# Moving x's transposes from once per batch to once per head pair, w2's bf16 copy into wd, and w2*w_out products to one lane

## The chip, the cores and the metric

The kernel runs on one core of a Trainium2 chip. The metric is device time in microseconds of one launch, the median of the timed runs. Five engines work side by side, each in its own program order: TensorE (PE; its weight loads are listed as PEld), VectorE (DVE), ScalarE (ACT), GpSimd (POOL) and SyncE (SP, which here only issues DMAs). They wait for each other through semaphores.

## The reference

Attention with queries averaged in pairs, then a maxout MoE layer on its output:

```python
B, H, S, D = 8, 8, 1152, 64
q_pool = q.reshape(B, H, S // 2, 2, D).mean(axis=3)
attn = softmax(q_pool @ k.T / sqrt(D))           # rows of 576 queries
attn_out = attn @ v                              # [8, 8, 576, 64]
x = attn_out.transpose(0, 2, 1, 3).reshape(4608, 512)
g = maximum(x @ w1, x @ w2)                      # w1, w2: 512 x 1024
out = g @ w_out                                  # w_out: 1024 x 512
```

All inputs and the output are fp32.

## The kernel before

It uses max(a, b) = max(a - b, 0) + b, so out = max(x (w1 - w2), 0) w_out + x (w2 w_out). Two bf16 matrices are made once: wd = w1 - w2 and w21 = w2 * w_out. The work is then of these kinds; letters are the queue names in the code.

- q, k: GpSimd casts a head pair's queries and keys (`qp` L353, `kbf` L329) and values (`vE` L367); queries and keys are transposed, for the first pairs on TensorE, later by DMA from SyncE's queue (L425, L342).
- Scores (L535) go to three, later two PSUM buffers `sps` in groups of 512 columns for both heads of a pair (the two halves of TensorE's rows at once). ScalarE's exponential (L542) turns each group into `et`. There are 324 groups over 32 head pairs.
- a: attention products per head, 45 matmuls of 65 columns (L384), with the row sum as an extra column. VectorE normalises: reciprocal (L473), multiply (L475), into `xnat`.
- x: `xnat` of a batch is transposed to `xT` (512 features in four blocks of 128 partitions, 4608 tokens). The first and the last batch are transposed on TensorE (`xtrans_pe`, L599, copied out at L605), batches 1 to 6 by DMA (`xtrans`, L585). Both start when all eight heads of a batch are normalised (`finish`, `x_wait`), in five pieces of tokens, 4 x 128 and 64, each of all 512 features.
- w: w2 is cast to bf16 (`w2b`, L626), transposed on TensorE (L641) to `w2T` (copied out at L647), and multiplied with w_out (`w21_jobs`, copied out at L660). wd is the subtraction L629. fp32 w2, w2b and w2T lie in the parts of `xT` that belong to later tokens, so x may be written there only when they have been read (`under`).
- h: max(x wd, 0) for 8 blocks of features (evacuated at L700, in the tail in part at L696).
- p: the output product of h with w_out plus x with w21, 12 matmuls per 128 tokens (evacuated at L729 or L726, stored from SyncE's queue at L676).

The order of all instructions is made before the launch. The `Plan` object keeps an estimate of each engine's free time and of when each operand will be seen; the loop `while p_end[0] < NTOK` picks the next unit for TensorE: scores when ScalarE has little queued, attention units before other work, MoE units (w, p, h) in what is left. `refill` turns queued jobs into running ones when a PSUM bank is free. While exponentials run, from group NARROW on, w, p and h jobs run as pairs, crossed: two jobs, each on one half of TensorE's rows at a time (L390); before it and in the tail they run whole (L384). Before NARROW there are two banks `fb` for everything but scores, then four, in the tail eight. A waiting instruction holds up all behind it on its engine.

Of the kernel before, what the change touches and what calls it, by code (L numbers as in the profile page):

```python
# [207 lines left out]
def bass_funnel_attn__then__act_maxout2_kernel(  # L208
# [32 lines left out]
    with ctx:  # L241
# [17 lines left out]
        rc = [sbuf([P, NCH + 1], FP32, f"rc{s}") for s in range(2)]  # L259
        xnat = [sbuf([P, NCH + 1, C], BF16, f"xnat{s}") for s in range(2)]  # L260
        xT = sbuf([P, NC_, NTOK], BF16, "xT")
# [109 lines left out]
        def unit(r, cost, go, mode="f"):  # L371
            return Unit(r, cost, mode, go=go)
# [81 lines left out]
        def av_jobs(i):  # L454
            b, h0 = i // NHP, 2 * (i % NHP)
            es = i % 2
            vs = i % 3
            xs = b % 2
            c0 = h0 * D
            need = [f"et{es}.{g - first(i)}" for g in range(first(i), after(i))] + [f"vE{vs}", "pad"]  # L460

            def chunk(half, sb):
                parts = []
                for t in range(NT):
                    a = (half * 2 + es) * PW + spot(i, t, sb * P)
                    parts.append((sb * 66, et[:, a:a + P], vE[vs][:, t, half, 0:65], t == 0, t == NT - 1))
                return parts

            def norm(half):
                def evac(m):  # L470
                    c = c0 + half * D
                    a = fb[m][:, 0:(NCH + 1) * 66].rearrange("p (j c) -> p j c", c=66)
                    dve(lambda e: e.reciprocal(rc[half][:, :], a[:, :, 64:65]),  # L473
                        [f"f{m}"], [f"rc{half}"], 0.19)
                    dve(lambda e: e.tensor_tensor(  # L475
                        xnat[xs][:, :, c:c + D], a[:, :, 0:D],
                        rc[half][:, :].unsqueeze(2).to_broadcast([P, NCH + 1, D]), ALU.mult),
                        [f"f{m}", f"rc{half}"],
                        [f"xn{xs}.{h0 + half}", f"f{m}"], 0.5)
# [82 lines left out]

        def place(b, j):

            if b % 2 == 0:
                return b * SQ + j * P
            return b * SQ + (NB + j * P if j < NCH else 0)

        def under(n0, n1):

            keys = [key for key, lo, hi in (("w2b", 512, 1536), ("w2T", 1536, 2560),
                                            ("w2f", 2560, NTOK)) if n0 < hi and lo < n1]
            if "w2T" in keys:
                keys += [f"w2T{ct}" for ct in range(NC_)]
            return keys

        def xsize(j):
            return P if j < NCH else NB

        def xtrans(b):  # L580
            xs = b % 2
            assert b == 0 or not queue["w"]
            for j in range(NCH + 1):
                n, n0 = xsize(j), place(b, j)
                op("SP", lambda e, n=n, n0=n0, j=j: e.dma_start_transpose(  # L585
                    xT[:, :, n0:n0 + n], xnat[xs][0:n, j, :]),
                    r=[f"xn{xs}.{h}" for h in range(H)], w=xkeys(n0, n0 + n),
                    after=under(n0, n0 + n), dma=f"d_x{xs}{j}", cost=0.65, mode="t")

        def xtrans_pe(b):  # L590
            xs = b % 2
            jobs = []
            for j in range(NCH + 1):
                n, n0 = xsize(j), place(b, j)

                def go(e, m, n=n, j=j):
                    mb = fb[m][:, :].bitcast(BF16)
                    for c in range(NC_):
                        last = e.transpose(mb[:, c * P:c * P + n],  # L599
                                           xnat[xs][0:n, j, c * P:(c + 1) * P], ident[0:n, 0:n])  # L600
                    return last

                def evac(m, n=n, n0=n0):
                    mb = fb[m][:, :].bitcast(BF16)[:, 0:NC_ * P].rearrange("p (c x) -> p c x", x=P)
                    op("DVE", lambda e: e.tensor_copy(xT[:, :, n0:n0 + n], mb[:, :, 0:n]),  # L605
                       r=[f"f{m}"], w=xkeys(n0, n0 + n) + [f"f{m}"], after=under(n0, n0 + n),
                       cost=0.4)
                jobs.append(Job("x", [unit([f"xn{xs}.{h}" for h in range(H)] + ["ident"],
                                           0.22 if n == P else 0.13, go, "f" if n == P else "s")],
                                evac))  # L610
            return jobs

        def xkeys(n0, n1):
            return [f"xT.{j}" for j in range(n0 // HP, n1 // HP)]

# [8 lines left out]
        def w_cast(part, ct):  # L624
            if part == 0:
                dve(lambda e: e.tensor_copy(w2b[:, ct, :], w2f[:, ct, :]),  # L626
                    [f"w2f{ct}"], [f"w2b{ct}", "w2b"], 0.6)
            elif part == 1:
                dve(lambda e: e.tensor_tensor(  # L629
                    wd[:, ct, :], w1f[:, ct, :], w2f[:, ct, :], ALU.subtract),  # L630
                    [f"w1f{ct}", f"w2f{ct}"], [f"wd{ct}", "w2f"], 1.2)
            else:
                dve(lambda e: e.tensor_copy(
                    wo[:, 2 * ct:2 * ct + 2, :], wof[:, 2 * ct:2 * ct + 2, :]),
                    [f"wof{ct}"], [f"wo{2 * ct}", f"wo{2 * ct + 1}"], 0.6)

        def w2t_job(ct):
# [7 lines left out]
            def evac(m):  # L645
# [3 lines left out]
                    [f"f{m}"], [f"w2T{ct}", "w2T", f"f{m}"], 1.15)  # L649
            return Job("w", [unit([f"w2b{ct}", "w2b", "ident"], 0.44, go)], evac)  # L650

# [16 lines left out]
        def store(lo, s, at):  # L668

            for half in range(2):  # L670
                n0 = lo + half * HP
                b, u = n0 // SQ, n0 % SQ
                if b % 2:
                    u = (u - NB) % SQ
# [9 lines left out]
        def h_jobs(n0, n1):  # L684
# [3 lines left out]
            for ft in range(NF):  # L688
                def part(ct, ft=ft):
                    return mm_unit([f"wd{ct}"] + [f"wo{j}" for j in range(NF)] + xkeys(n0, n1), 0.216 * size / 512, [  # L690
                        (0, wd[:, ct, ft * P:(ft + 1) * P], xT[:, ct, n0:n1], ct == 0, ct == NC_ - 1)])
# [14 lines left out]
        def p_job(lo, at=slice(0, E)):  # L706
# [3 lines left out]
            def part(j):  # L710
                if j < NC_:
                    lhs, rhs = xT[:, j, lo:hi], w21[:, j, at]
                    r = [f"w21{j}"] + xkeys(lo, hi)
                else:
# [118 lines left out]
        def flush():  # L833
# [24 lines left out]
            for b in list(x_wait):  # L858
                if b in X_PE:
                    x_wait.remove(b)  # L860
                    queue["x"].extend(xtrans_pe(b))
                elif plan.ops[plan.writer[f"xn{b % 2}.{H - 1}"]]["seen"] <= now():
                    x_wait.remove(b)
                    xtrans(b)

# [18 lines left out]
        def more_moe():  # L884
            tail = nxt == NGR
            keys = [f"wd{ct}" for ct in range(NC_)] + [f"wo{ft}" for ft in range(NF)]
            while h_at[0] < NTOK and not queue["h"] and all(key in plan.writer for key in keys):
                n0 = h_at[0]
                most = min(HB - n0 % HB, p_end[0] + RING - n0, NTOK - n0)
                n1 = n0  # L890
                while n1 < n0 + most and all(key in plan.writer for key in xkeys(n1, n1 + HP)) and plan.when(
                        "PE", r=xkeys(n1, n1 + HP)) <= now() + (9.0 if tail else 0.05):
                    n1 += HP
# [25 lines left out]
        def refill():  # L919
# [232 lines left out]
```

## Time and profile before

| | us |
|---|---|
| timed runs, median of 3 | 381.17 (380.3 to 381.26) |
| profiled execution, own time | 379.94 |
| its span on the core | 378.2 |
| TensorE busy | 360.4 (95%) |
| ScalarE busy | 317.6 (84%) |
| GpSimd busy | 162.4 (43%) |
| VectorE busy | 139.9 (37%) |

The span is cut into rows by engine, line and tile. TensorE's busy time is modelled at its ends, so a TensorE at 95% is not one at its peak. TensorE's clock was at full speed throughout. An idle time in brackets is that of the engine just ahead of the row, with what ended it.

### The profile page before, as it was taken

The page shows a single profiled execution, that of the slowest core. Times are in us where ns is not written, and L with a number is a line of the kernel's source. Part 1 is how long each engine was busy: PE and PEld are TensorE (multiplying, and loading weights), DVE is VectorE, ACT ScalarE, POOL GpSimd, SP SyncE. Part 2 cuts the span into 40 slices and gives each one's busy share as a digit, 9 for nine tenths or more (in the row PEclk, how much of TensorE's full clock was granted, in tenths as well). Part 3 has the DMA queues.
Part 4 walks back from the last instruction along what each step waited for, and adds up shares of the span by engine and source line. Part 5 has one row for each costly group of instructions (what it writes and reads, how often), then busy time and mean ns, then how long its engine had stood idle before and what let it go on. Part 6 is the DMA issues. An engine that isn't in the chain of part 4 may idle for free.

```text
span 378.2 us, 13193 instructions
## 1 busy us (share of the span) xinstructions
PE 360.4 (95%) x5928; PEld 232.0 (61%) x5928; DVE 139.9 (37%) x323; ACT 317.6 (84%) x359; POOL 162.4 (43%) x135
## 2 busy tenths in 40 slices
PE   4798999899999999999999999999999999999996
PEld 2464566667665656666666666666656666676554
DVE  3256963314234242422343333241424243353221
ACT  5999989899989999999999899899999999932221
POOL 2855597575445554655155634555437110000000
PEclk9999999999999999999999999999999999999999
DMA  8999999999999999999999998999999772031423
GB/s 285 406 391 401 383 280 322 248 352 293 249 193 270 326 307 143 334 307 251 166 282 245 310 257 237 290 260 271 167 280 266 128 90 50 3 67 37 95 55 83
DMA packets 93816, 88.69 MB, mean 235 GB/s; under 512 B 66112, under 2 KB 66880, under 8 KB 93760
## 3 DMA queue, kind: packets, MB, share of 16 engines
q1 hardware_dynamic: 93328, 87.46, 90.9%
q8 instruction: 46, 0.75, 0.8%
q10 hardware_dynamic: 432, 0.39, 0.4%
q14 instruction: 10, 0.08, 0.1%
HBM read 62.91 MB, written 9.44 MB: 191 GB/s over the span
## 4 chain that ended last, share of the span: by engine, by line
PE 83%; ACT 5%; DMA 4%; DVE 3%; issue 2%; POOL 2%; POOLq 0%
PE sps L535 18%; PE sps L384 18%; PE sps L390 16%; PE fb L384 16%; PE fb L390 13%; ACT et L542 5%; DMA vraw<-in_v_dram 3%; POOL qp L353 1%; DVE wd L629 1%; DMA kraw<-in_k_dram 1%; DVE stage L729 1%; PE fb L438 1%; DVE stage L700 1%; POOL vE L367 0%; PE fb L599 0%
## 5 line engine op out<-in xcount | busy, mean ns | idle before, releaser
L542 ACT ACTIVATE et<-sps 128x1024 bf16<-128x1024 f32 (+1 forms) x336 | 306.2, 1011 | 20.9 <-PE sps L535 18.7
L535 PE MATMUL sps<-qpT,kT 64*128 64x256 bf16 (+7 forms) x1162 | 120.6, 288 | 6.1 <-ACT et L542 4.9
L353 POOL TENSOR_TENSOR qp<-qraw 64x576 bf16<-64x576 f32 x62 | 88.2, 1423 | 47.3 <-DMA qpT<-qp 37.2
L535 PEld LDWEIGHTS sps<-qpT,kT 64*128 64x128 bf16 x1162 | 47.1, 95 | 52.6 <-ACT et L542 23.5
L367 POOL TENSOR_SCALAR vE<-vraw 128x1152 bf16<-128x1152 f32 x32 | 38.0, 1187 | 85.6 <-PE fb L384 43.0
L384 PEld LDWEIGHTS fb<-vE,et 128*128 128x128 bf16 x1710 | 54.4, 97 | 11.9 <-issue 5.9
L384 PE MATMUL fb<-vE,et 128*128 128x65 bf16 x1710 | 60.4, 193 | 0.5 <-DVE w L660 0.3
L384 PEld LDWEIGHTS sps<-vE,et 128*128 128x128 bf16 x1170 | 37.1, 97 | 7.1 <-issue 3.4
L329 POOL TENSOR_SCALAR kbf<-kraw 128x1152 bf16<-128x1152 f32 x31 | 35.7, 1150 | 13.3 <-DMA kraw<-in_k_dram 11.0
L384 PE MATMUL sps<-vE,et 128*128 128x65 bf16 x1170 | 40.6, 193 | 0.0
L390 PE MATMUL fb<-xT,wd 64*128 64x384 bf16 (+3 forms) x448 | 39.0, 279 | 1.2 <-DVE stage L729 0.9
L700 DVE TENSOR_SCALAR stage<-sps 128x384 bf16<-128x384 f32 (+3 forms) x57 | 24.8, 468 | 29.9 <-PE sps L390 21.6
L390 PE MATMUL sps<-xT,wd 64*128 64x384 bf16 (+3 forms) x368 | 34.3, 293 | 0.5 <-DVE stage L729 0.2
L390 PE MATMUL sps<-wo,stage 64*128 64x512 bf16 x256 | 34.8, 376 | 0.0
L700 DVE TENSOR_SCALAR stage<-fb 128x384 bf16<-128x384 f32 (+3 forms) x57 | 22.9, 441 | 30.9 <-PE fb L390 29.9
L473 DVE RECIPROCAL rc<-fb 128x5 f32<-128x5 f32 x38 | 7.4, 195 | 59.3 <-PE fb L384 59.3
L390 PEld LDWEIGHTS fb<-xT,wd 64*128 64x128 bf16 x448 | 19.2, 94 | 11.2 <-PE fb L390 1.3
L729 DVE COPY stage<-sps 128x512 f32<-128x512 f32 (+1 forms) x19 | 12.1, 673 | 31.9 <-PE sps L390 21.5
L390 PE MATMUL fb<-wo,stage 64*128 64x512 bf16 x160 | 21.9, 376 | 0.0
L390 PEld LDWEIGHTS sps<-xT,wd 64*128 64x128 bf16 x368 | 15.7, 94 | 9.9 <-DVE xnat L475 1.1
L473 DVE RECIPROCAL rc<-sps 128x5 f32<-128x5 f32 x26 | 5.1, 195 | 43.7 <-PE sps L384 43.7
L726 ACT COPY stage<-sps 128x512 f32<-128x512 f32 (+1 forms) x5 | 2.7, 543 | 22.1 <-PE sps L384 22.1
(59 smaller groups left out, 239.6 us busy)
## 6 DMA issues: line engine op xcount, KB each, us to landing
vraw<-in_v_dram SPq DMA_DIRECT2D x32, 576.0 KB, 7.6
kraw<-in_k_dram SPq DMA_DIRECT2D x31, 576.0 KB, 6.3
qraw<-in_q_dram SPq DMA_DIRECT2D x31, 576.0 KB, 5.7
out_dram<-stage SPq DMA_DIRECT2D x70, 128.0 KB, 3.4
xT<-in_moe_w_dram SPq DMA_DIRECT2D x4, 512.0 KB, 11.8
stage<-in_moe_w_out_dram SPq DMA_DIRECT2D x4, 512.0 KB, 15.2
stage<-in_moe_w_dram SPq DMA_DIRECT2D x4, 512.0 KB, 12.8
xT<-xnat SPq DMA_TRANSPOSE x30, 5.3
```

Of the source, the lines that this page charges most:

```text
L329: op("POOL", lambda g: g.tensor_scalar(kbf[s][:, :, :, :].rearrange("p t h d -> p h t d"), kraw[r][:, :, :, :], 1.0, 1.0, ALU.mult, ALU.mu ...
L353: op("POOL", lambda g, half=half, a=a: g.tensor_tensor(qp[s][:, :, half, :], a[:, :, 0, :], a[:, :, 1, :], ALU.add), r=[f"qraw{r}"], w=[f" ...
L367: op("POOL", lambda g: g.tensor_scalar(vE[r][:, :, :, 0:D].rearrange("p t h d -> p h t d"), vraw[r][:, :, :, :], 1.0, 1.0, ALU.mult, ALU.m ...
L384: last = e.matmul(fb[ms[0]][:, at:at + rhs.shape[-1]], lhs, rhs, start=start, stop=stop)
L390: last = e.matmul(fb[m][:, at:at + rhs.shape[-1]], lhs[rows(half)], rhs[rows(half)], start=first, stop=fin)
L438: last = e.transpose(mb[:, (t - lo) * P:(t - lo + 1) * P], kbf[s][:, t, :, :].rearrange("p h d -> p (h d)"), ident[:, :])
L473: dve(lambda e: e.reciprocal(rc[half][:, :], a[:, :, 64:65]), [f"f{m}"], [f"rc{half}"], 0.19)
L535: last = e.matmul(sps[r][:, h, col:col + hi - lo], kT[i % 3][rows(h), t, :], qpT[i % 3][rows(h), lo:hi], start=True, stop=True)
L542: op("ACT", lambda e: e.activation(et2[:, :, c:c + z - a], sps[r][:, :, a - g * W:z - g * W], EXP, scale=scale), r=[f"s{r}"], w=keys + [f" ...
L629: dve(lambda e: e.tensor_tensor(wd[:, ct, :], w1f[:, ct, :], w2f[:, ct, :], ALU.subtract), [f"w1f{ct}", f"w2f{ct}"], [f"wd{ct}", "w2f"], 1.2)
L700: dve(lambda e: e.tensor_scalar_max(gT[:, ft, g0:g0 + size], fb[m][:, 0:size], 0.0), [f"f{m}"], w, 0.1 + size / 960.0)
L729: dve(lambda e: e.tensor_copy(osb[o][:, 0:n], fb[m][:, 0:n]), [f"f{m}"], [f"osb{o}", f"f{m}"], 0.1 + n / 966.0)
```

## The change

Three edits.

1. x is transposed per head pair. `xnat` is laid out as [partition, pair, token chunk, 128], so that a pair's 128 features lie together. `finish` queues a pair as soon as its two heads are normalised. On TensorE (batches 0 and 7) a pair is one unit of five 128 x 128 transposes and one copy of 128 x 576; in the other batches it is one DMA of five blocks, 640 columns wide. The last 64 columns of that DMA fall on the next batch's first tokens, which are written later (keys `spill`). Tokens keep their order in `xT` for odd batches too (`place` is gone). Readers of xT now wait per block of features.
2. w2b lies in wd's room instead of a part of xT. The subtraction that fills a quarter of wd comes after that quarter of w2 has been transposed.
3. Of the w2*w_out products, one job (or pair of jobs) runs at a time.

```diff
-        xnat = [sbuf([P, NCH + 1, C], BF16, f"xnat{s}") for s in range(2)]
+        xnat = [sbuf([P, NHP, NCH + 1, P], BF16, f"xnat{s}") for s in range(2)]
...
-        w2b = xT[:, :, 512:1536]
+        w2b = wd
...
-                        xnat[xs][:, :, c:c + D], a[:, :, 0:D],
+                        xnat[xs][:, i % NHP, :, half * D:half * D + D], a[:, :, 0:D],
...
-        def xtrans(b):
-            xs = b % 2
-            assert b == 0 or not queue["w"]
-            for j in range(NCH + 1):
-                n, n0 = xsize(j), place(b, j)
-                op("SP", lambda e, n=n, n0=n0, j=j: e.dma_start_transpose(
-                    xT[:, :, n0:n0 + n], xnat[xs][0:n, j, :]),
-                    r=[f"xn{xs}.{h}" for h in range(H)], w=xkeys(n0, n0 + n),
-                    after=under(n0, n0 + n), dma=f"d_x{xs}{j}", cost=0.65, mode="t")
+        def xtrans(i):
+            b, pr = i // NHP, i % NHP
+            xs, n0 = b % 2, b * SQ
+            assert b < 2 or not queue["w"] and all(run.job.kind != "w" for run in running)
+            op("SP", lambda e: e.dma_start_transpose(
+                xT[:, pr, n0:n0 + XW].rearrange("p (j x) -> p j x", x=P),
+                xnat[xs][:, pr, :, :].rearrange("p j c -> p (j c)")),
+                r=[f"xn{xs}.{2 * pr + half}" for half in range(2)],
+                w=xkeys(n0, n0 + SQ, [pr]) + [f"spill{pr}"],
+                after=under(n0, n0 + XW), dma=f"d_x{xs}{pr}", cost=0.85, mode="t")
...
+        def xtrans_pe(i):
+            b, pr = i // NHP, i % NHP
+            xs, n0 = b % 2, b * SQ
+
+            def go(e, m):
+                mb = fb[m][:, :].bitcast(BF16)
+                for j in range(NCH + 1):
+                    last = e.transpose(mb[:, j * P:(j + 1) * P], xnat[xs][:, pr, j, :], ident[:, :])
+                return last
+
+            def evac(m):
+                mb = fb[m][:, :].bitcast(BF16)
+                op("DVE", lambda e: e.tensor_copy(xT[:, pr, n0:n0 + SQ], mb[:, 0:SQ]),
...
-            return [f"xT.{j}" for j in range(n0 // HP, n1 // HP)]
+            return [f"xT.{j}.{ct}" for j in range(n0 // HP, n1 // HP) for ct in cts]
...
             elif part == 1:
+                assert f"w2T{ct}" in plan.writer
                 dve(lambda e: e.tensor_tensor(
                     wd[:, ct, :], w1f[:, ct, :], w2f[:, ct, :], ALU.subtract),
-                    [f"w1f{ct}", f"w2f{ct}"], [f"wd{ct}", "w2f"], 1.2)
+                    [f"w1f{ct}", f"w2f{ct}"], [f"wd{ct}", f"w2b{ct}", "w2f"], 1.2)
...
                     if wide and kind == "p" and "p" in kinds:
                         break
+                    if kind == "w" and "w" in kinds and queue[kind][0].split:
+                        break
...
-                b = job.nb // NHP
-                if all(av_half.get(b * NHP + j) == 2 for j in range(NHP)):
-                    x_wait.append(b)
+                if av_half[job.nb] == 2:
+                    x_wait.append(job.nb)
```

More of the change, by code (lines that the diff above doesn't have):

```diff
@@ L458, in av_jobs @@
             xs = b % 2
-            c0 = h0 * D
             need = [f"et{es}.{g - first(i)}" for g in range(first(i), after(i))] + [f"vE{vs}", "pad"]
@@ L470, in evac @@
                 def evac(m):
-                    c = c0 + half * D
                     a = fb[m][:, 0:(NCH + 1) * 66].rearrange("p (j c) -> p j c", c=66)
@@ L561, in bass_funnel_attn__then__act_maxout2_kernel @@
         K_CUT = 4
[L563 to L567, printed above, removed]
         def under(n0, n1):
-            keys = [key for key, lo, hi in (("w2b", 512, 1536), ("w2T", 1536, 2560),
+            keys = [key for key, lo, hi in (("w2T", 1536, 2560),
                                             ("w2f", 2560, NTOK)) if n0 < hi and lo < n1]
@@ L590, in xtrans_pe @@
[L590 to L611, printed above, removed]
@@ L613, in xkeys @@
-        def xkeys(n0, n1):
-            return [f"xT.{j}" for j in range(n0 // HP, n1 // HP)]
+        XW = (NCH + 1) * P
+        def xtrans(i):
[8 more added lines that the diff above has]
+                after=under(n0, n0 + XW), dma=f"d_x{xs}{pr}", cost=0.85, mode="t")
@@ new lines, in xtrans_pe @@
+        def xtrans_pe(i):
[9 more added lines that the diff above has]
+                op("DVE", lambda e: e.tensor_copy(xT[:, pr, n0:n0 + SQ], mb[:, 0:SQ]),
+                   r=[f"f{m}"], w=xkeys(n0, n0 + SQ, [pr]) + [f"f{m}"],
+                   after=under(n0, n0 + SQ) + [f"spill{pr}"], cost=0.46)
+            return Job("x", [unit([f"xn{xs}.{2 * pr + half}" for half in range(2)] + ["ident"], 0.28, go)],
+                       evac)
@@ L616, in w_load, with xkeys @@
+        def xkeys(n0, n1, cts):
+            return [f"xT.{j}.{ct}" for j in range(n0 // HP, n1 // HP) for ct in cts]
         def w_load(part, c):
@@ L626, in w_cast @@
                 dve(lambda e: e.tensor_copy(w2b[:, ct, :], w2f[:, ct, :]),
-                    [f"w2f{ct}"], [f"w2b{ct}", "w2b"], 0.6)
+                    [f"w2f{ct}"], [f"w2b{ct}"], 0.6)
             elif part == 1:
+                assert f"w2T{ct}" in plan.writer
                 dve(lambda e: e.tensor_tensor(
                     wd[:, ct, :], w1f[:, ct, :], w2f[:, ct, :], ALU.subtract),
-                    [f"w1f{ct}", f"w2f{ct}"], [f"wd{ct}", "w2f"], 1.2)
+                    [f"w1f{ct}", f"w2f{ct}"], [f"wd{ct}", f"w2b{ct}", "w2f"], 1.2)
             else:
@@ L649, in evac @@
                     [f"f{m}"], [f"w2T{ct}", "w2T", f"f{m}"], 1.15)
-            return Job("w", [unit([f"w2b{ct}", "w2b", "ident"], 0.44, go)], evac)
+            return Job("w", [unit([f"w2b{ct}", "ident"], 0.44, go)], evac)
         def w21_jobs():
@@ L672, in store @@
                 b, u = n0 // SQ, n0 % SQ
-                if b % 2:
-                    u = (u - NB) % SQ
                 eng = "ACT" if half and lo + P == NTOK else "SP"
@@ L689, in part @@
                 def part(ct, ft=ft):
-                    return mm_unit([f"wd{ct}"] + [f"wo{j}" for j in range(NF)] + xkeys(n0, n1), 0.216 * size / 512, [
+                    return mm_unit([f"wd{ct}"] + [f"wo{j}" for j in range(NF)] + xkeys(n0, n1, [ct]), 0.216 * size / 512, [
                         (0, wd[:, ct, ft * P:(ft + 1) * P], xT[:, ct, n0:n1], ct == 0, ct == NC_ - 1)])
@@ L712, in part @@
                     lhs, rhs = xT[:, j, lo:hi], w21[:, j, at]
-                    r = [f"w21{j}"] + xkeys(lo, hi)
+                    r = [f"w21{j}"] + xkeys(lo, hi, [j])
                 else:
@@ L857, in flush @@
                     store(*held.pop(o))
[L858 to L864, printed above, removed]
+            for i in list(x_wait):
+                if i // NHP in X_PE:
+                    x_wait.remove(i)
+                    queue["x"].append(xtrans_pe(i))
+                elif plan.ops[plan.writer[f"xn{i // NHP % 2}.{2 * (i % NHP) + 1}"]]["seen"] <= now():
+                    x_wait.remove(i)
+                    xtrans(i)
         def more_banks(g, m):
@@ L890, in more_moe @@
                 n1 = n0
-                while n1 < n0 + most and all(key in plan.writer for key in xkeys(n1, n1 + HP)) and plan.when(
-                        "PE", r=xkeys(n1, n1 + HP)) <= now() + (9.0 if tail else 0.05):
+                while n1 < n0 + most and all(key in plan.writer for key in xkeys(n1, n1 + HP, range(NC_))) and plan.when(
+                        "PE", r=xkeys(n1, n1 + HP, range(NC_))) <= now() + (9.0 if tail else 0.05):
                     n1 += HP
```

2 lines of the change are left out of this document (removed).

## The prediction

> **What bounds the kernel now.** I read the page first, then the list of waits, then ScalarE's timeline, then the last 45 us of TensorE's weight loads, which show when each matmul run starts.
>
> ```profile
> span 378.2 us, 13193 instructions
> PE 360.4 (95%) x5928; PEld 232.0 (61%) x5928; DVE 139.9 (37%) x323; ACT 317.6 (84%) x359; POOL 162.4 (43%) x135
> ...
> PE 83%; ACT 5%; DMA 4%; DVE 3%; issue 2%; POOL 2%; POOLq 0%
> ...
> L542 ACT ACTIVATE et<-sps 128x1024 bf16<-128x1024 f32 (+1 forms) x336 | 306.2, 1011 | 20.9 <-PE sps L535 18.7
> ```
>
> TensorE is busy 95% of the span and holds 83% of the chain that ended last, but ScalarE has 306.2 us of exponentials (L542) and only 20.9 us of idle ahead of them. Whether one engine waits for the other or both take turns is in the waits:
>
> ```profile
> PEld sps L535 <- ACT et L542: 23.5, 77, 1.0
> ACT et L542 <- PE sps L535: 18.7, 34, 1.4
> ```
>
> Both: TensorE stops 77 times for a score bank that ScalarE has not read yet, ScalarE stops 34 times for scores. ScalarE's timeline shows where (start, length, merged run, and in brackets the idle ahead of it):
>
> ```profile
> 43.46 5.92 ACT L542 ACTIVATE et<-sps 128x1024 bf16<-128x1024 f32 x7 [0.66 <-PE sps L535]
> 49.76 5.72 ACT L542 ACTIVATE et<-sps 128x1024 bf16<-128x1024 f32 x6 [0.38 <-PE sps L535]
> 56.50 4.69 ACT L542 ACTIVATE et<-sps 128x1024 bf16<-128x1024 f32 x5 [1.02 <-PE sps L535]
> ...
> 70.96 9.45 ACT L542 ACTIVATE et<-sps 128x1024 bf16<-128x1024 f32 x10 [1.36 <-PE sps L535]
> ...
> 203.88 8.73 ACT L542 ACTIVATE et<-sps 128x1024 bf16<-128x1024 f32 x10 [0.51 <-PE sps L535]
> 213.46 10.36 ACT L542 ACTIVATE et<-sps 128x1024 bf16<-128x1024 f32 x11 [0.85 <-PE sps L535]
> ...
> 326.52 6.71 ACT L542 ACTIVATE et<-sps 128x1024 bf16<-128x1024 f32 x7 [0.56 <-PE sps L535]
> ```
>
> So there are two stages. Up to 333 us the exponentials set the pace: about ten of them, then an idle of some 0.5 us where the attention products of a head (a run of 45 matmuls) hold TensorE. MoE work fills the gaps. From 333 us no exponentials are left, and TensorE works off what MoE is left. The end therefore moves by two things: MoE work taken out of the tail, and idle of ScalarE added or removed before it.
>
> **The tail.** The order of the built programs can be compared without times. After the last score group both have 90 attention matmuls and the same 132 matmuls of the output product. Before, there follow 40 matmuls of x with wd of 384 columns, 64 of 192, 16 crossed ones of 384 (two 64-row halves side by side) and x's transposes in units of 4, 4, 8 and 4. The change leaves 32, 64, 8 crossed, and one transpose unit of 5: three of the last batch's four head pairs are transposed earlier, under the exponentials.
>
> ```profile
> 331.61 0.64 PEld L390 LDWEIGHTS fb<-xT,wd 64*128 64x128 bf16 x8
> ...
> 337.13 0.32 PEld L599 LDWEIGHTS sps<-ident,xnat 128*128 128x128 bf16 x4 [0.23 <-DVE xnat L475]
> ...
> 338.14 0.34 PEld L599 LDWEIGHTS sps<-ident,xnat 128*128 128x128 bf16 x4
> ...
> 338.99 0.60 PEld L599 LDWEIGHTS sps<-ident,xnat 128*128 128x128 bf16 x8
> ...
> 342.81 0.14 PEld L599 LDWEIGHTS sps<-ident,xnat 64*128 64x128 bf16 x3 [0.16 <-issue]
> ...
> 343.68 0.61 PEld L384 LDWEIGHTS sps<-xT,wd 128*128 128x128 bf16 x8 [0.32 <-DVE xT L605]
> ...
> 362.54 3.08 PEld L384 LDWEIGHTS sps<-xT,wd 128*128 128x128 bf16 x19
> ```
>
> Eight matmuls of 384 columns at 3.08/19 = 0.162 us are 1.30 us; eight crossed ones are 0.64 us. Transposes: 0.32 + 0.34 + 0.60 + 0.14 = 1.40 us, of which one unit of five (some 0.40) stays, so 1.00 us goes; of the waits of 0.23 and 0.32 the first stays, the second may go, and I leave it out. Rounded down a little for prefetched loads that overlap other runs: **-2.8 us** (bounds -2.0, the two matmul terms alone, and -3.3). Nothing covers this work, since TensorE runs end to end in the tail.
>
> **x of a batch comes late today.** Five transposes leave SyncE's queue back to back only once all eight heads of a batch are done:
>
> ```profile
> 96.97 7.90 SPq L585 DMA_TRANSPOSE xT<-xnat  x5
> ...
> 108.19 0.31 PEld L390 LDWEIGHTS fb<-xT,wd 64*128 64x128 bf16 x8 [1.18 <-DVE stage L729]
> ...
> L585 SPq DMA_TRANSPOSE xT<-xnat x30: 1192/1292/2449, 97.0 to 304.6; - x30
> ...
> L342 SPq DMA_TRANSPOSE kT<-kbf x27: 1244/2567/4771, 43.8 to 307.2; - x27
> ...
> xT<-xnat SPq DMA_TRANSPOSE x30, 5.3
> ```
>
> In the built order the run at 108.19 waits for the first and last of these five and for VectorE; the last is issued near 103.3 and lands 5.3 us later, about 108.6. So I read the 1.18 us as the wait for x, though the profile names VectorE. With the change three quarters of a batch are in place long before, one transpose is left after the last head, and each product waits for its own head pair only. **-0.7 us** (bounds -1.2 and 0: ScalarE had work queued for part of it, and the other batches show no such stall).
>
> SyncE issues 24 transposes instead of 30, each of five blocks. Their issue is not in this trace; it lies between 1.29 us (four blocks, L585) and 2.57 us (nine blocks, L342): 31 to 62 us in all against 39 us. I take the lower end, being one block from it. Each is one issue ahead of a pair's q and k transposes, where before a burst of 7.90 us stood there once per batch without a matmul waiting for q or k. That slack hides it; without it, every pair's scores could come up to 2.6 us late.
>
> **The start.** w2 in bf16 now lies in wd, so a wd subtraction (L629) may run only after that quarter of w2 is transposed; the built order shows this satisfied in time. But VectorE's queue changes: a subtraction now stands ahead of a normalisation (L473, L475) that it followed, and copies of x stand between.
>
> ```profile
> 38.31 2.01 DVE L633 CAST wo<-stage 128x1024 bf16<-128x1024 f32 x3
> 40.27 0.20 DVE L473 RECIPROCAL rc<-fb 128x5 f32<-128x5 f32 x1
> 40.49 0.49 DVE L475 TENSOR_TENSOR xnat<-fb,rc 128x320 bf16<-128x320 f32 x1
> 40.90 1.22 DVE L629 TENSOR_TENSOR wd<-stage,xT 128x1024 bf16<-128x1024 f32 x1
> ...
> 43.12 4.08 DVE L629 TENSOR_TENSOR wd<-stage,xT 128x1024 bf16<-128x1024 f32 x2
> 47.12 0.68 DVE L660 CAST w<-fb 128x512 bf16<-128x512 f32 x1
> 47.72 1.82 DVE L629 TENSOR_TENSOR wd<-stage,xT 128x1024 bf16<-128x1024 f32 x1
> ...
> 42.63 1.15 POOL L329 TENSOR_SCALAR kbf<-kraw 128x1152 bf16<-128x1152 f32 x1 [4.06 <-DMA kraw<-in_k_dram]
> ...
> L629 DVE TENSOR_TENSOR wd<-stage,xT x4: 1215/1778/2422, 40.9 to 47.7; 128x1024 bf16<-128x1024 f32 x4
> ...
> 47.85 1.41 PEld L384 LDWEIGHTS fb<-vE,et 128*128 128x128 bf16 x45 [0.61 <-DVE w L660]
> ```
>
> The new order, from 38.4: two casts of 0.67, subtraction 1.22, normalisation 0.7, subtraction 1.22, normalisation 0.7, subtraction 2.04, copy of x about 0.46, subtraction 1.82, copy L660 0.68. That ends at 48.6 instead of 47.8, and the attention run at 47.85, which needs the bank that this copy frees, starts 0.75 us later; the score groups and exponentials queue behind it. Against that, the idle of 1.02 us ahead of 56.50 follows a gap into which the old order puts twelve transposes of x and eight w2*w_out products; the new order has six of those products and six crossed ones of x there, and the transposes lie in earlier gaps, so I take a third of that idle, 0.35 us, as gone. **+0.4 us** (bounds -0.5 and +1.6).
>
> I put 1.22 on the first two subtractions because the one here ran while GpSimd stood idle until 42.63, and 1.8 to 2.0 on those after it. The Trainium skill, "SBUF — State Buffer", section "SBUF: two separate sides", says why: a VectorE instruction with two SBUF inputs and a GpSimd instruction that reads SBUF take a shared port pair from each other for a whole instruction. By that rule, which these rows bear out, the delay is 0.75; by the group's mean of 1.78 for all four it would be 1.6.
>
> **The middle.** What leaves the tail enters the gaps: 9216 crossed columns of wd products (1.9 us) and fifteen transposes. Where TensorE has time left that is free. Where it lengthens a run between two score groups, ScalarE runs dry: a full attention run alone costs 0.51 to 0.56; with four crossed products of 384 ahead (0.32 us) the idle at 213.46 is 0.85; with fourteen narrower ones at 70.96 it is 1.36. So what stands ahead of an attention run costs about its own length. The new order has four such runs in the middle (about 0.65, 0.43, 0.33, 0.16 us) where the old has three (0.32, 0.08, 0.08): 1.57 - 0.48 = **+1.1 us** (bounds 0 and +2.1, all the moved work).
>
> **Sum.** -2.8 - 0.7 + 0.4 + 1.1 = -2.0 us against the profiled execution's 379.94 us (span 378.2 and 1.74 around it): 377.9. The three timed runs have a median of 381.17, 1.23 above it; on that scale **379.2 us**. About 0.3% (1.1 us) is what a measurement can tell from no change, so this is not far beyond it.
>
> **Rivals.** (a) *The moved work is free and the waits go too*: the middle and the start cost nothing, -2.8 - 1.2 - 0.5 = -4.5, 376.7 us. For it: 23.5 us of TensorE's waits for ScalarE. Against: they are short, and most are early. (b) *The gain is given back under the exponentials*: tail at its lower bound -2.0, x's wait hidden by queued exponentials (0), start +0.8, middle +1.1: about 0, 381.1 us. For it: the waits for x show up clearly once only. (c) *Slower: TensorE has no room in the middle.*
>
> ```profile
> 160.00:190.00 30.00, 30.00 (x516) 18.78 (x514) 8.95 (x21) 28.12 (x31) 12.52 (x11) 1.00 1.15 245
> ```
>
> Between 160 and 190 us TensorE is busy 30.00 of 30.00 us. Then each moved microsecond comes back whole (+2.1) and the longer attention runs starve ScalarE on top (+1.1), with the start at +1.6: 4.8 - 2.8 - 0.3 = +1.7, 382.9 us. It decides from the point at which ScalarE's idle between 43 and 333 us grows by over 2.8 us. Against it: ScalarE's own pace, not TensorE's load, sets the ten-exponential rhythm, and idle stays near 0.5 per head pair in busier and emptier stretches alike.
>
> **Numbers.** Forecast 42%, (a) 18%, (b) 24%, (c) 16%: faster 0.60, same 0.24, slower 0.16. The range runs from 376.9, just inside (a), to 382.0, short of (c)'s end.
>
> **What would show it.** Right: the last score group some 0.5 to 1 us later than 331.6, the time from there to the end shorter by nearly 3 us, one transpose unit in the tail, no idle of TensorE near 108, L629 still near 1.8 us. Wrong: ScalarE's idle ahead of L542 over 23.7 us (20.9 + 2.8), then (c); under 20, then (a); matmuls of scores that wait for q's or k's transposes, then SyncE's queue had no slack.

## The result, and the profile after

| | before | after |
|---|---|---|
| median of the timed runs, us | 381.02 (380.3 to 381.26) | 385.62 (384.93 to 386.94) |
| profiled execution: own time, span | 379.94, 378.2 | 385.84, 384.1 |
| TensorE busy + idle = span | 360.4 + 17.8 | 362.5 + 21.6 |
| exponentials end, tail from there | 333.2, 45.0 | 342.2, 41.9 |

The ratio is 1.0128, interval 1.0097 to 1.0159: slower by 4.9 us. Ratios here leave out executions over 1.5% above the fastest of their kernel; where times spread wider than that, the median of all is given too.

The page of the kernel after, the lines that answer to those quoted of before:

```profile
span 384.1 us, 13179 instructions
PE 362.5 (94%) x5928; PEld 232.9 (61%) x5936; DVE 140.6 (37%) x322; ACT 316.9 (83%) x358; POOL 162.1 (42%) x135
...
PE 79%; DMA 9%; ACT 6%; DVE 3%; SPq 1%; issue 1%; POOL 1%
...
L540 ACT ACTIVATE et<-sps 128x1024 bf16<-128x1024 f32 (+1 forms) x336 | 306.1, 1010 | 29.9 <-PE sps L533 27.7
```

The exponentials took as long as before (306.1 us), but ScalarE's idle ahead of them grew from 20.9 to 29.9. Those 9.0 us are the 9.0 by which the attention stage ends later. The tail gave 3.1 back. The list of waits after (total, times, longest):

```profile
ACT et L540 <- PE sps L533: 27.7, 39, 3.8
PEld sps L533 <- ACT et L540: 26.9, 99, 0.8
...
PE fb L390 <- DMA xT<-xnat: 5.4, 2, 4.0
```

The last row is new: before had no row of TensorE waiting for x's DMA. TensorE's timeline after shows both places (start, length, merged run, idle ahead of it):

```profile
101.65 0.25 PE L390 MATMUL fb<-xT,wd 64*128 64x192 bf16 x2
105.91 0.82 PE L390 MATMUL fb<-xT,wd 64*128 64x192 bf16 x10 [4.02 <-DMA xT<-xnat]
106.58 0.38 PE L533 MATMUL sps<-qpT,kT 64*128 64x256 bf16 x4
106.89 2.53 PE L384 MATMUL sps<-vE,et 128*128 128x65 bf16 x45
...
190.19 0.26 PE L390 MATMUL fb<-xT,wd 64*128 64x192 bf16 x2 [1.43 <-DMA xT<-xnat]
```

The unit that stands is the fourth feature block of a crossed h pair: the product with the last head pair of batch 1 (then of batch 3). Scores and attention units queue behind it, so ScalarE runs dry. Why x is late there, from SyncE's timeline after:

```profile
91.63 3.47 SPq L342 DMA_TRANSPOSE kT<-kbf  x1
95.16 3.14 SPq L662 DMA_DIRECT2D out_dram<-stage  x4
98.34 0.59 SPq L309 DMA_DIRECT2D qraw<-in_q_dram  x1
99.40 0.38 SPq L301 DMA_DIRECT2D kraw<-in_k_dram  x1
99.83 1.25 SPq L575 DMA_TRANSPOSE xT<-xnat  x1
```

The pair was normalised at 95.24. Four stores and two loads stood ahead in the queue, the transpose was issued at 99.83 and was there for the matmul at 105.91, 10.7 us after the normalisation. The planner, when it wrote TensorE's order, counted it as seen at 96.5 on its own clock, which has the normalisation at 90.3: it allowed 6.1 us. Behind the wait the clock falls (windows after: length, busy time of each engine with counts, granted clock, DMA share, GB/s):

```profile
103.20:106.60 3.40, 0.62 (x12) 0.46 (x14) 0.00 (x0) 0.00 (x1) 0.00 (x0) 1.00 1.12 301
106.70:110.00 3.30, 3.30 (x57) 2.79 (x53) 1.13 (x4) 1.02 (x1) 0.00 (x0) 0.56 1.17 349
```

With the clock at 0.56 the attention run of 45 matmuls took 2.53 us, where 1.53 is usual.

### The profile page after: what moved, and what is told of

Read it like the earlier page. It is cut to its first block, busy times and chain, and to the rows that moved or that the text cites. A ratio compares the mean times of both kernels' runs of the same rounds, so it can differ in the third digit from the quotient of the medians.

```text
span 384.1 us, 13179 instructions
## 1 busy us (share of the span) xinstructions
PE 362.5 (94%) x5928; PEld 232.9 (61%) x5936; DVE 140.6 (37%) x322; ACT 316.9 (83%) x358; POOL 162.1 (42%) x135
## 4 chain that ended last, share of the span: by engine, by line
PE 79%; DMA 9%; ACT 6%; DVE 3%; SPq 1%; issue 1%; POOL 1%
PE sps L384 20%; PE sps L533 17%; PE fb L390 16%; PE fb L384 14%; PE sps L390 10%; ACT et L540 6%; DMA qraw<-in_q_dram 4%; DMA xT<-xnat 3%; DVE wd L617 1%; DMA kraw<-in_k_dram 1%; SPq L662 1%; POOL qp L353 1%; DVE xnat L473 1%; PE fb L589 0%; DVE stage L686 0%
## 5 line engine op out<-in xcount | busy, mean ns | idle before, releaser
L540 ACT ACTIVATE et<-sps 128x1024 bf16<-128x1024 f32 (+1 forms) x336 | 306.1, 1010 | 29.9 <-PE sps L533 27.7
L384 PE MATMUL sps<-vE,et 128*128 128x65 bf16 x1530 | 53.8, 194 | 0.0
L384 PEld LDWEIGHTS fb<-vE,et 128*128 128x128 bf16 x1350 | 43.7, 98 | 10.1 <-issue 4.1
L384 PE MATMUL fb<-vE,et 128*128 128x65 bf16 x1350 | 48.1, 194 | 0.8 <-DVE w L648 0.8
L686 DVE TENSOR_SCALAR stage<-sps 128x384 bf16<-128x384 f32 (+1 forms) x67 | 28.0, 452 | 36.6 <-PE sps L390 27.0
L390 PE MATMUL sps<-xT,wd 64*128 64x384 bf16 (+1 forms) x448 | 40.8, 286 | 0.2
L390 PE MATMUL fb<-xT,wd 64*128 64x384 bf16 (+1 forms) x384 | 35.0, 287 | 5.8 <-DMA xT<-xnat 5.4
L390 PE MATMUL fb<-wo,stage 64*128 64x512 bf16 x288 | 39.9, 376 | 0.0
L686 DVE TENSOR_SCALAR stage<-fb 128x384 bf16<-128x384 f32 (+1 forms) x48 | 20.1, 461 | 24.0 <-PE fb L390 23.9
L715 DVE COPY stage<-fb 128x512 f32<-128x512 f32 x19 | 12.3, 687 | 29.0 <-PE fb L390 24.4
L390 PE MATMUL fb<-w,xT 64*128 64x512 bf16 x144 | 21.0, 376 | 0.1
L390 PEld LDWEIGHTS fb<-wo,stage 64*128 64x128 bf16 x288 | 13.4, 94 | 9.4
## 6 DMA issues: line engine op xcount, KB each, us to landing
stage<-in_moe_w_out_dram SPq DMA_DIRECT2D x4, 512.0 KB, 15.1
```

The source lines that it names most:

```text
L384: last = e.matmul(fb[ms[0]][:, at:at + rhs.shape[-1]], lhs, rhs, start=start, stop=stop)
L390: last = e.matmul(fb[m][:, at:at + rhs.shape[-1]], lhs[rows(half)], rhs[rows(half)], start=first, stop=fin)
L540: op("ACT", lambda e: e.activation(et2[:, :, c:c + z - a], sps[r][:, :, a - g * W:z - g * W], EXP, scale=scale), r=[f"s{r}"], w=keys + [f" ...
L686: dve(lambda e: e.tensor_scalar_max(gT[:, ft, g0:g0 + size], fb[m][:, 0:size], 0.0), [f"f{m}"], w, 0.1 + size / 960.0)
L715: dve(lambda e: e.tensor_copy(osb[o][:, 0:n], fb[m][:, 0:n]), [f"f{m}"], [f"osb{o}", f"f{m}"], 0.1 + n / 966.0)
```

## The experiments

Theory 1: TensorE's fixed order asks for x before it has landed, since the planner counts it too early. Theory 2: the half clock behind thin stretches and stands is a cost of its own. Theory 3, the prediction's rival (c) made general: TensorE has no room, so whatever comes into the middle comes back whole. Each ratio is to the kernel before on the same chip (its medians there: 381.6 us for e1 to e4, 382.2 for e5 to e8, 381.7 for e9 to e12, 381.9 for e13 to e16).

**e1: the late transpose moved up SyncE's queue.** The fence shows the order of the queue, not code.

```diff
 L342 kT transpose
+L575 x transpose, batch 1, last pair
 L662 four stores, L309 q load, L301 k load
-L575 x transpose, batch 1, last pair
```

> The changed kernel with one thing moved: on SyncE's queue the transpose of batch 1's last pair goes ahead of the four stores and two loads that stood before it; the order on the other four engines is the changed kernel's. Theory 1 (late x: TensorE, in its fixed order, stands 4.0 us at 101.9 us for this transpose, and the slow clock follows from that stand): the transpose is issued behind the kT transpose at about 95.2 instead of 99.8 us, lands near 101 to 102, the wait of 4.0 us falls under 1, the half-clock stretch at 106.7 goes, ScalarE's idle time ahead of the exponentials falls from 29.9 to 23 to 26 us, and the time from 385.6 to between 380.5 and 382.5. Rival theory 3 (TensorE has no room for the work that has come into the middle): the wait only turns into waits further on, ScalarE's idle time stays over 28 us and the time within 1 us of 385.6.

Measured 386.8 us, ratio 1.0126 (1.0101 to 1.0152): no gain. SyncE's (the last pairs of batches 1 and 2) and then TensorE's timeline of e1:

```profile
94.71 3.26 SPq L575 DMA_TRANSPOSE xT<-xnat  x1
...
141.35 1.59 SPq L575 DMA_TRANSPOSE xT<-xnat  x1
```

```profile
99.85 0.99 PE L390 MATMUL fb<-xT,wd 64*128 64x192 bf16 x12
...
142.57 0.65 PE L390 MATMUL fb<-xT,wd 64*128 64x384 bf16 x6
149.78 0.50 PE L390 MATMUL fb<-xT,wd 64*128 64x384 bf16 x2 [6.56 <-DMA xT<-xnat]
```

The wait at 102 us is gone as theory 1 said, but TensorE then stood 6.56 us for the last pair of batch 2, which had not stood before. It came to that product near 143.2 us, where the changed kernel comes to it at 149.77, but that pair's transpose was issued at 141.35 against 142.08, hardly earlier, and landed 8.4 us after its issue. Theory 1's time was missed, theory 3's met (ScalarE's idle ahead of the exponentials is 32.0 us), and by theory 1's mechanism: one order, and each batch's last pair is a place where it may be too early.

**e2: the early gap filled.**

```diff
+                    if i == 3 and hi == NT:
+                        for n in range(8):
+                            last = e.matmul(fb[m][:, 256:512], ident[:, :], kbf[s][:, 0:2, :, :].rearrange(
+                                "p t h d -> p (t h d)"), start=True, stop=True)
```

> The changed kernel with eight more matmuls (128x128 by 256 columns, results never read) behind the second group of k transposes for pair 3, at about 26 us, where TensorE then stands 0.87 us for the q of that pair. Theory 2 (the clock: TensorE runs little but transposes from 24.7 to 28.1 us and is then granted half its clock for the next 3.4 us, which starves ScalarE): with the gap filled the granted clock in 28 to 32 us goes from 0.57 to 0.9 or more, ScalarE's idle time between 28 and 43 us from 1.9 to under 0.6, and the time falls by 1 to 2 us to 383.6 to 384.6. Rival (the early idle time comes from the new order itself, or TensorE has no room): about 0.85 us of matmuls are added, the clock stays or the idle time stays, and the time is 385.6 to 386.6.

Measured 386.9 us, ratio 1.0122 (1.0085 to 1.016). The clock between 28.2 and 31.5 us was 1.00 instead of 0.56, and ScalarE did not stand there. But in e1, which has no filling, that stretch had full clock too, so the filling is not shown to be the reason, and the time did not fall, against theory 2: the wait for x at batch 1 was 8.0 us in e2's profile.

**e3: without the pairwise x.** The kernel before with edits 2 and 3 (edit 3 alone leaves TensorE's order of the kernel before as it was).

```diff
-        w2b = xT[:, :, 512:1536]
+        w2b = wd
...
+                    if kind == "w" and "w" in kinds and queue[kind][0].split:
+                        break
```

> The kernel before with w2 in w1-w2's room and the one lane for the w2*w_out jobs, but x transposed by batch as before. Theory 1 puts the loss on the pairwise x (5.4 us of waits for x and the slow clock behind the longer of them): without it no wait for x is longer than the 1.2 us of before, the tail stays at about 45 us, and what is left is the early thin stretch with its slow clock, so 381 to 383. Rival theory 3 (the work set free by the early w2*w_out fills TensorE too full in the middle): the idle time of ScalarE grows by 4 us or more here too, and the time is 385 or more, since the tail is not shortened.

The ratio is 1.0047 (1.0012 to 1.0081), but the times lie in two groups, four from 380.7 to 382.8 and eight from 384.9 to 387.6, median of all 385.7, 1.1% over before. The profiled execution was one of the lower group (382.76). No row of it names x, but at 108.35 us TensorE stands 1.76 us ahead of the first product of batch 1, with VectorE named. The kernel before stands there too:

```profile
108.22 0.51 PE L390 MATMUL fb<-xT,wd 64*128 64x192 bf16 x8 [0.93 <-DVE stage L729]
```

So theory 1 in its first form, that only the pairwise x brings the waits, does not follow; e11 takes this up.

**e4: x counted as landing 5 us later by the planner.**

```diff
-            seen = self.dma_free + 0.7
+            seen = self.dma_free + 0.7 + lag
...
-                after=under(n0, n0 + XW), dma=f"d_x{xs}{pr}", cost=0.85, mode="t")
+                after=under(n0, n0 + XW), dma=f"d_x{xs}{pr}", cost=0.85, mode="t", lag=5.0)
```

> The changed kernel whose planner counts each x transpose over the DMA queue as landing 5 us later than it did (96.5 becomes 101.5 for batch 1's last pair; the trace has about 105.9), so that work on it is put later in TensorE's order. Theory 1: both waits for x (4.0 and 1.4 us) fall to under 1.5 in sum, no half-clock stretch near 107, ScalarE's idle time ahead of the exponentials 21 to 25 us, time 379 to 381.5. Rival theory 3: the middle is too full whatever the order; ScalarE's idle time stays over 28 us, and the time is 384 to 387.

Measured 382.48 us, ratio 1.0023 (0.9993 to 1.0054): most of the loss is gone. Waits for x are 2.1 us, ScalarE's idle ahead of the exponentials is 23.7. As theory 1 said, at a time one us above its range.

**e5 and e6: no wait for x, in the order of after and of before.** The products of batches 1 to 6 take batch 0's columns of xT in place of their own, so the output of those batches is not the reference's. The cut from e5:

```diff
-                        (0, wd[:, ct, ft * P:(ft + 1) * P], xT[:, ct, n0:n1], ct == 0, ct == NC_ - 1)])
+                        (0, wd[:, ct, ft * P:(ft + 1) * P], xT[:, ct, own(n0, size):own(n0, size) + size], ct == 0, ct == NC_ - 1)])
...
+        for o in plan.ops:
+            if o["eng"] == "PE":
+                o["deps"] = {d for d in o["deps"] if not (plan.ops[d]["dma"] or "").startswith("d_x")}
```

> The changed kernel, instruction by instruction in its order, but the gated jobs and the output jobs of batches 1 to 6 take batch 0's columns of xT as data (so the output of those batches is not the reference's) and TensorE waits for no x transpose; all transposes are still issued and moved. Theory 1 (the loss is TensorE standing for x, and the slow clock behind it): no wait for x is left, ScalarE's idle time ahead of the exponentials falls from 29.9 to 21 to 25 us, the time from 385.6 to 379.5 to 382. Theory 3 (TensorE is as good as full from end to end, so the work that the shorter tail gave up lengthens the attention stage by as much): most of the loss stays, 383.5 to 385.5. Both at once: the attention stage ends 3 us later than before's 333.2, the tail is 3 us shorter, and the time is that of before, 381 to 382.

> The same taken from the kernel before: its order, batch 0's columns of xT as data for the gated and output jobs of batches 1 to 6 (so the output of those is not the reference's), no wait of TensorE for x. Its profile has one such wait of 1.2 us at 108 us. If TensorE's standing time passes whole into the time, 0.8 to 1.2 us are gained (380.4 to 380.8 where before has 381.6); if ScalarE has slack behind it, nothing to 0.4 us.

e5: 379.34 us, ratio 0.9927 (0.9899 to 0.9956). e6: 380.76 us, ratio 0.9961 (0.9938 to 0.9985). The page of e5 and the end of its exponentials in ScalarE's timeline:

```profile
span 376.7 us, 13198 instructions
PE 361.6 (96%) x5928; PEld 233.1 (62%) x5936; DVE 140.0 (37%) x322; ACT 316.4 (84%) x358; POOL 162.2 (43%) x135
...
L540 ACT ACTIVATE et<-sps 128x1024 bf16<-128x1024 f32 (+1 forms) x336 | 305.6, 1011 | 22.9 <-PE sps L533 20.7
```

```profile
327.16 7.61 ACT L540 ACTIVATE et<-sps 128x1024 bf16<-128x1024 f32 x8 [0.47 <-PE sps L533]
```

Same order, same DMAs, only no wait for x: TensorE's idle falls from 21.6 to 15.1 us, the exponentials end at 334.8 instead of 342.2, the tail stays 41.9. The waits and what follows them cost the changed kernel 1.0128 - 0.9927 = 2.0%, 7.7 us, and the kernel before 0.4%, 1.5 us (its idle at 108 us, which the profile puts down to VectorE, is gone in e6). By the intervals of the ratios, the difference of 6.2 us is uncertain by about 2. Theory 1 holds; theory 3 does not explain the loss.

**e7: more work for TensorE in the kernel before.**

```diff
+                again = b in (3, 4) and sb == 0
-                for t in range(NT):
+                for t in range(NT) if not again else list(range(NT)) * 2:
```

> The kernel before with the first nine matmuls of each attention-times-V job of batches 3 and 4 done twice (16 jobs by 9 by 34 ns, 4.9 us more on TensorE inside the attention stage; the results are the same). Theory 3 (TensorE has no room in the middle, so that its busy and standing time add up to the span): 4 to 5.5 us slower, 385.6 to 387. What the prediction took (moved work costs the middle about a third of its length, since ScalarE's exponentials set the pace there): 0 to 2 us slower, 381.6 to 383.6.

Measured 387.02 us, ratio 1.0125 (1.0094 to 1.0157): 4.8 us for 4.9 us of matmuls, as theory 3 said. But its profile has TensorE standing 2.74 us at 110.18, ahead of the first product of batch 1, where the kernel before stands 0.93 and none of the added work has come yet. So some 1.8 us of the 4.8 may be a longer wait for x, and the added matmuls lengthen attention runs, whose length the prediction had charged in full as well. That TensorE has no room anywhere in the middle is not shown.

**e8, e12, e13, e16: the changed kernel with 8, 6, 8 again and 7 us; e14, e15: the kernel before with 8 and 5 us.** The edit is that of e4 with another number; in the kernel before it stands on L585.

> As the run with 5 us, but each x transpose counted as landing 8 us later, near the 9.4 us by which batch 1's last pair was late. Theory 1: no wait of TensorE for x over 0.5 us, ScalarE's idle time ahead of the exponentials 20 to 23 us, time 380 to 382. Theory 3: the work put off comes back in the tail, which is then 45 us or more as before, and the time is within 1 us of 382.5, the time with 5 us; no gain over before by either, unless TensorE's busy time falls under the 360 us that before has.

> As the runs with 5 and 8 us, with 6 us. With 5 us 2.1 us of waits for x were left; with 8 us none were, but TensorE ran out of work near 105 and 150 us. Theory 1 puts the best between them: waits for x under 1 us, 379.8 to 381.5 and no slower than before. Theory 3: within 0.5 us of the time with 8 us, since only TensorE's busy time counts, which is the same.

> The changed kernel with each x transpose counted as landing 8 us later, again. Theory 1 (the loss was the due time, the change itself is a small gain): 0.1 to 0.5% faster than before, as the first time. Theory 3 (the change is worth nothing either way): within 0.3% of before, and no better than the kernel before with the same due times.

> The kernel before with each x transpose counted as landing 8 us later. Its profile has 1.2 us of waits for x, and without them it is 0.4% faster; a later due time takes the waits away but moves work toward the tail. Theory 1: it gains less than that, 0 to 0.3%, or loses by a longer tail (tail 45 us or more, time 381 to 383), and stays behind the changed kernel with the same due time. Rival (the later due time is all that helped): it is as fast as the changed kernel with 8 us, 380 to 381.

> The same with 5 us. Theory 1: between before and its run without waits, 380.4 to 382.5; behind the changed kernel with 8 us. Rival: as fast as the changed kernel with 8 us or faster.

> The changed kernel with 7 us. With 5 and 6 us one wait for x of 1.2 to 1.5 us was left (382.5, 382.6), with 8 none (380.9). Theory 1: 380.5 to 382.5, the lower end if no wait for x is left in its profile, the upper if one is; no slower than with 6.

| | us | ratio to before | waits for x in its profile |
|---|---|---|---|
| changed, 5 us (e4) | 382.48 | 1.0023 (0.9993 to 1.0054) | 2.1 |
| changed, 6 us (e12) | 382.61 | 1.0029 (1.0001 to 1.0057) | 1.5 |
| changed, 7 us (e16) | 381.49 | 1.0005 (0.9978 to 1.0032) | 0.8 |
| changed, 8 us (e8) | 380.87 | 0.9972 (0.9946 to 0.9998) | none |
| changed, 8 us (e13) | 380.88 | 0.9984 (0.9961 to 1.0007) | none |
| before, 5 us (e15) | 382.70 | 1.0024 (0.9995 to 1.0053) | none |
| before, 8 us (e14) | 385.31 | 1.0082 (1.0045 to 1.012) | none |

The later the due time, the less TensorE waits for x. With 8 us the changed kernel is at before's time or a little better; only the first of its two intervals excludes no change. The later due time is not what helps by itself: with 8 us it makes the kernel before slower. Theory 1's ranges were missed in three of these runs, each time on the slow side: e12 by 1.1 us, with a wait for x left in its profile, e14 by 2.3, whose cause is open, and e15 by 0.2. The price shows in e8: the tail is 44.7 us again, as theory 3 said, and TensorE runs out of work where it stood before. TensorE's timeline of e8:

```profile
105.94 0.39 PE L533 MATMUL sps<-qpT,kT 64*128 64x512 bf16 x2 [0.42 <-ACT et L540]
106.86 0.39 PE L533 MATMUL sps<-qpT,kT 64*128 64x64 bf16 x4 [0.52 <-ACT et L540]
107.77 0.39 PE L533 MATMUL sps<-qpT,kT 64*128 64x128 bf16 x4 [0.53 <-ACT et L540]
```

**e9 and e10: the wait filled with matmuls, beside the changed kernel.**

```diff
...
+        def filled(e, fn=ahead["fn"]):
+            fn(e)
+            for n in range(32):
+                last = e.matmul(fb[0][:, 256:512], ident[:, :], wd[:, 0, 0:256], start=False, stop=False)
+            return last
...
```

> The changed kernel with 32 matmuls (128x128 by 256 columns, about 3.4 us, results never read) put on TensorE directly ahead of the unit that stands 4.0 us for batch 1's last x transpose; everything else is the changed kernel. It prices the clock alone, the wait being as long as before. Theory 2 (the half clock that follows the stand costs TensorE half of 3.4 us): no stretch at half clock from 106.7 to 110.1 us, time 385.6 to 383.3 to 384.6. Rival (the slow clock costs nothing beside the wait, since ScalarE is then behind anyway): 385 to 386.5; slower than that only if the wait in most executions is shorter than the filling.

> The changed kernel itself beside the others on the same chip. Every theory: 1.0 to 1.6% over before, 385 to 387; by theory 1 its profile has one wait for x of 3 to 8 us at a batch's last pair, at whichever batch, and by theory 2 a stretch of 3.4 us at half clock behind it.

e9: 388.03 us, ratio 1.0181 (1.0145 to 1.0218). e10: 387.53 us, ratio 1.0135 (1.0094 to 1.0176). TensorE's timeline and two windows of e9:

```profile
101.88 3.67 PE L1096 MATMUL fb<-wd,ident 128*128 128x256 bf16 x32
105.48 0.83 PE L390 MATMUL fb<-xT,wd 64*128 64x192 bf16 x10
106.14 0.38 PE L533 MATMUL sps<-qpT,kT 64*128 64x256 bf16 x4
106.45 1.53 PE L384 MATMUL sps<-vE,et 128*128 128x65 bf16 x45
...
188.97 0.34 PE L390 MATMUL fb<-xT,wd 64*128 64x192 bf16 x2 [2.14 <-DMA xT<-xnat]
```

```profile
104.00:108.00 4.00, 3.94 (x76) 3.18 (x75) 0.62 (x2) 1.02 (x1) 0.00 (x0) 1.00 1.20 213
...
188.00:192.00 4.00, 3.03 (x49) 2.61 (x50) 0.00 (x0) 1.02 (x1) 0.00 (x0) 0.57 1.27 208
```

Locally theory 2 is right: with TensorE kept busy the clock stayed at 1.00 and the attention run took 1.53 us instead of 2.53. But the next wait for x was longer than the one after has there (2.14 against 1.43 us), and the half clock came behind that one. The time did not fall, theory 2's was missed, and what the slow clock alone costs stays open. e10 shows the changed kernel's waits at the same two places, longer than in its first profile (5.58 and 3.46 us); the profiled execution is the slowest of its six, 390.18 us.

**e11: e3 without waits for x** (the edit of e5 on e3).

> The kernel with the other two edits and x by batch (whose times lay in two groups, 381 to 383 and 385 to 388), now with batch 0's columns of xT as data for the gated and output jobs of batches 1 to 6 (so the output of those is not the reference's), so that TensorE waits for no x. Theory 1 (the upper group are executions in which x lands late and TensorE stands for it): one group only, 379 to 382.5, as narrow as that of before. Rival (the upper group comes from the early thin stretch and its slow clock): two groups stay, with some executions at 385 or more.

Measured 380.55 us, all from 378.9 to 382.0, ratio 0.9965 (0.9942 to 0.9987). The upper group of e3 is gone, as theory 1 said: edits 2 and 3 alone are enough to bring TensorE's order to x too early in most executions. No execution of that group was profiled, so where it stands is not shown. Without waits, edits 2 and 3 are worth nothing beside e6 (0.9965 against 0.9961); e5's 0.9927 has the pairwise x in addition, though the intervals overlap.

## Why the prediction was wrong

- **Tail, -2.8: right.** 45.0 to 41.9 us, -3.1, and the same from e6 to e5; one transpose unit was left in it.
- **x of a batch comes late today, -0.7: the step that failed.** "With the change three quarters of a batch are in place long before, one transpose is left after the last head, and each product waits for its own head pair only." All of that holds, and the wait grew. The step looked at when x lands, and not at where the new order puts the product that needs the last pair. The planner moved the products up too, to its own idea of when that pair lands: at batches 1 and 3, the two where TensorE stands, its plan has TensorE there 0.6 us after the pair counts as seen. At the other batches it leaves 3.0 us or more, and in the kernel before it left 3.8 at batch 1. From normalisation to use the planner allowed 6.1 us at batch 1 and 5.2 at batch 3, the trace took 10.7 (4.6 of them ahead of the issue) and 7.4. Less what the planner allowed and the 0.6, about 4.0 and 1.6 us are left, and TensorE stood 4.0 and 1.4. (The 9.4 us of e8's expectation are not all lateness: the planner's clock is 4.9 us ahead of the trace's at that point.) The 1.2 us of before became 5.4 to 9.0 us in the two profiles. By e5 and e6 the waits cost 7.7 us after and 1.5 before, so the term was +6.2 instead of -0.7.
- **SyncE's queue, nothing.** No score waited for a transposed q or k by DMA, as I said, and x's issues took 1.28 us in the median, the lower end as taken. I had asked only what x's transposes hold up, not what holds them up: at batch 1, 4.6 us of stores and loads.
- **Start, +0.4: the wrong place.** ScalarE stood 0.2 us between 20 and 43 us before, 1.4 in e5, 2.0 after (with the clock at 0.56 from 28.2 us). That is 1.2 to 1.8 more, the latter past the upper bound of 1.6, and earlier than the prediction had it. Between 43 and 60 us, its place, ScalarE was busy 15.09 us before, 15.26 in e5 and 15.22 after: nothing was lost there, though in the changed kernel TensorE did wait 0.78 us for the copy L648 (0.34 before). L617 took 1.735 us in the mean, the first two 1.22, as expected.
- **Middle, +1.1: not shown by itself.** Start and middle together were +1.5. Without waits for x, the exponentials end 2.0 us later in e5 than in e6 (332.8 us). Since 1.2 us or so were lost ahead of 43 us, less is left for the middle than the prediction gave it. TensorE's idle in the first 43 us fell from 10.1 us before to 7.9 in e5; that moved work went there, and so came cheap, is argued and not shown.
- **The sum without x.** Tail, start and middle made -1.3 us. e5 against e6 measures 0.9927/0.9961, -1.3 us; each ratio is uncertain by 0.3% and the start was misplaced, so the closeness is luck, but these terms were not what failed. With +6.2 in place of -0.7 the sum is +4.9, as measured; that is the same agreement once more, since the 6.2 was taken from the same ratios.
- **Rivals.** (c) had the side right and its mark was passed (29.9 us of idle against 23.7), but at 382.9 it was 2.7 us short, and its mechanism, work without room, is not what made the loss: that mark cannot tell it from TensorE standing for x. A rival in which x lands after TensorE has come to it was missing: with +6.2 for its term it would have stood at 386.

## What to carry to other kernels

When an order is written at build time from estimated landing times, an operand that arrives earlier also pulls its readers earlier: at each place where the order leans on it, compare the time that the planner allows from the operand's making to its use with the same time in the trace (their clocks may be apart), before counting a wait as gone. Where one engine is busy 95% of the span, add up its busy and its idle time; a wait removed at one place is only a gain if no later operand is then met too early (e1). A kernel that reads other data in place of the late operand prices all such waits at once.

## What the runs showed of the hardware

- A TensorE that had stood for 4.0 us was granted 0.56 of its clock over the next 3.3 us, and in e10, after 5.6 us, 0.50; 45 attention matmuls took 2.53 us instead of 1.53. The Trainium skill, "TensorE: Matmul & The Clock Gate", Part 1, section "What's actually happening", has half rate after an idle window of about 3.4 us, with windows that run free of the kernel; these rows agree. A thin stretch, 2.20 busy of 3.40 us from 24.7, was followed by 0.56 in the changed kernel and a like one (2.12) by 1.00 in e1.
- x's transposes by DMA took 5.3 us in the median from issue to landing before (four blocks), 6.0 after and 7.2 in e8 (five blocks).
